# FFN in chunks of 128, 128 and then 256 tokens, w_down loaded in pieces, five weight slabs, and another order of the first loads

## The chip, the cores and the metric

The kernel runs on one core of one Trainium2 chip. The metric is the device time of one execution in microseconds, from the first to the last instruction with what lies around them; a run is one execution, and the time of a kernel is the median of its runs. Profiles come from one further execution.

## The reference

One pre-norm transformer block over 2048 tokens, width 1024, in bf16. Attention has 32 query heads of width 32 that share one key and one value head; the feed-forward part (FFN) has width 3584 and a sigmoid gate.

```python
def _A_ref(x, wq, wk, wv, wo):                 # x: 1 x 2048 x 1024
    q = (x @ wq).reshape(B, S, H, Dh).transpose(0, 2, 1, 3)      # H = 32, Dh = 32
    k = x @ wk
    v = x @ wv
    scores = jnp.einsum("bhqd,bkd->bhqk", q, k) * (Dh ** -0.5)
    p = softmax(scores, axis=-1)
    o = jnp.einsum("bhqk,bkd->bhqd", p, v)
    return o.transpose(0, 2, 1, 3).reshape(B, S, H * Dh) @ wo

def _B_ref(x, w_gate, w_up, w_down):           # F = 3584
    h = sigmoid(x @ w_gate) * (x @ w_up)
    return h @ w_down

h = x + _A_ref(layernorm(x), wq, wk, wv, wo)
out = h + _B_ref(layernorm(h), w_gate, w_up, w_down)
```

## The kernel before

**A planner writes the order.** The kernel doesn't list its instructions by hand. Each operation is an `Op` with an engine, the operations that it depends on, and an assumed cost (`t_act`, `t_dve`, `t_mm`, for DMAs an issue cost `occ` and bytes over a rate). A `Plan` runs a list scheduler over them with those assumed costs, and keeps for each engine one list. When it is done, every engine gets its list as a fixed program, in that order, with semaphore waits where an operation depends on another engine. So the chip follows the planned order whatever the true durations are; an instruction that waits holds up all behind it on its engine. Operations for ACT, DVE, POOL and SP are taken by readiness and then priority. PE's list is made by the loop at line 683, which decides at each moment between a block of scores and other matmuls.

**Tokens** go in 16 tiles of 128. The stages:

- *Head.* x is loaded in 16 tiles into `x_sb` on ACT's DMA queue (line 238), between them wk, wv, the two halves of wq and wo (242 to 260). Per tile (or pair of tiles) DVE takes the statistics (`stats`, line 270), POOL makes the reciprocal deviation with two powers, DVE subtracts the mean (311), and ACT (tiles 1 to 9) or DVE (the others) scales (319, 315). SP then transposes the tile by DMA into `xnT` (322). POOL copies wk four times side by side into `wk4` (266), so that keys come out in four row groups.
- *KV and Q.* `mk_KV` makes keys and values of a pair of tiles, `mk_Q` queries of one group of four heads. The first 512 tokens' queries stay in SBUF (`QTb`), in groups of 256 tokens; the others are made in groups of 512 tokens, copied to `qst` (which lies in `hact`), stored to a DRAM scratch (397) and loaded again per chunk of 256 tokens (416).
- *Attention.* 512 *visits*: for tile and head group (`G` = tile x 8 + group) and a quarter of the keys, `emit_S` issues 16 score matmuls, four at a time in four row groups, and ACT takes two exponentials of 128 x 1024 (line 478). Four visits make one group's probabilities; then `mk_PV` multiplies them by the values (64 matmuls of 33 columns, the last column giving the sum), and DVE divides (511, 513). A tile's eight groups are transposed by DMA into `OT` (519), and `mk_OP` multiplies by wo, adds x, takes the second layer norm's statistics and writes `hn` (302). Visits 0 to 31 belong to tile 0, 32 to 63 to tile 1, and so on, the first two groups interleaved.
- *FFN.* `hn` is transposed by DMA into `hnT` (579), which holds one chunk. For each chunk of 256 tokens (`c`, 8 of them) and each of 28 tiles of F, `mk_GU` does 8 gate and 8 up matmuls of 256 columns into one PSUM bank; ACT takes tanh (620; sigmoid is written with it), DVE multiplies into `hactT` (627). The weights come in *slabs* of 256 columns of F, gate and up, 512 KB each, into a ring of four (`wgu`, `load_slab`, line 588), which all chunks load anew; a slab is loaded when the last matmul on its space is done. `mk_D` then does the down projection, four groups of 28 matmuls of 512 columns, adds h (659) and stores (662).

**Space that is shared.** `wd_sb` (w_down, 7 MB) lies over `zone`, where `xnT`, wq, wk and wv are: it is loaded in four pieces when the last query group is done (line 400). `x_sb` lies over the slab ring: slab s waits until the transposes of tiles 4s to 4s+3 have landed (line 672).

**What may run when.** Two PSUM banks (`F_ps`) serve all groups but the scores. PE takes the first class in `PRIO` whose queue has a group that is ready: KV, Q0, PV, OP, D, GU, Q. A score block goes first if ACT has under 750 ns of work waiting. A chunk's GU groups need all queries done (chunk 0) or the chunk before wholly through D (`gr.gate`, 642); their transposes need both tiles' `hn` and the last GU matmul of the chunk before (`flush_hT`, 576). So chunk c needs tiles 2c and 2c+1 through attention.

The numbers of visits that the prediction uses come from the order of PE's instructions in the built programs. Before: OP of tile 1 ends at visit 72, GU of chunk 0 runs in visits 77 to 120 and its D in 120 to 144, OP of tile 3 ends at 140, chunk 1 starts at 146, chunk 6 at 486. After the last score block stand, in this order: 34 GU matmuls, 64 of PV, 64 GU, 16 OP, 96 GU, 112 D, 448 GU, 112 D.

The softmax here doesn't subtract the row's maximum and nothing guards it: scores larger than these inputs give would overflow.

## Time and profile before

| | us |
|---|---|
| runs | 1210.52, 1211.20, 1210.39 |
| median | 1210.52 |
| the profiled execution's own time | 1211.99 |
| its span, first to last instruction | 1210.2 |
| PE busy | 1148.6 (95%) |
| ACT busy | 1037.1 (86%) |
| DVE busy | 287.8 (24%) |
| ACT: 1024 exponentials, busy | 974.7, 1037 ns each |
| PE: 3584 GU matmuls, busy | 440.8 |
| DMA | 163.56 MB, 135 GB/s over the span |
| DMA queue of ACT (loads of the head) | 8.52 MB |
| slab loads | 224 of 512 KB, all on SP |

Busy time is the time in which an engine has at least one instruction under way; consecutive instructions overlap in their pipelines, so 1037 ns is the length of one exponential, while the spacing of consecutive ones is less. PE's share of 95% says that it almost always has something under way, not that it runs at its peak. The chain of waits follows the work that ended last back from the end, and is the view that says which engine's speed set the end in each stage.

### The profile page before, as it was taken

To read this page: it belongs to the slowest core of one execution; us is meant where nothing else is said; L and a number is where in the kernel's file an instruction comes from. 1 tells how busy PE (TensorE), PEld (TensorE's weight loads), DVE (VectorE), ACT (ScalarE), POOL (GpSimd) and SP (SyncE) were. 2 spreads that over 40 slices of the span, in tenths; PEclk is the share of its full clock that TensorE was granted. 3 is DMA by queue.
4 is the path that set the end of the run, shared out by engine and by line. 5 is a ranking of instruction groups with operands and counts; after the bars stand their busy time and mean duration, and the time that the engine had idled before them with its cause. 6 is when DMAs were issued, how large, how long until landed. Compare 5 with 4: busy or idle time off the path is not lost.

```text
span 1210.2 us, 46354 instructions
## 1 busy us (share of the span) xinstructions
PE 1148.6 (95%) x21632; PEld 812.1 (67%) x21632; DVE 287.8 (24%) x762; ACT 1037.1 (86%) x1281; POOL 39.4 (3%) x86
## 2 busy tenths in 40 slices
PE   0899957999999999999999999999999999999999
PEld 0655545877577866777577866787568865787684
DVE  8222302221122212221212121222122221222121
ACT  1679998999999999999999999999999999991120
POOL 4100000000000000000000000000000000000000
PEclk9999957999999999999999999999999999999999
DMA  9941271666146541657236660576326750569390
GB/s 314 195 97 46 63 263 28 182 159 179 42 117 170 162 129 29 182 152 197 43 83 158 175 154 24 133 195 184 63 63 176 182 141 15 115 177 239 111 251 18
DMA packets 309297, 163.56 MB, mean 135 GB/s; under 512 B 57968, under 2 KB 299632, under 8 KB 309104
## 3 DMA queue, kind: packets, MB, share of 16 engines
q1 hardware_dynamic: 301600, 152.07, 48.8%
q10 hardware_dynamic: 7504, 8.52, 2.1%
q8 instruction: 170, 2.79, 1.0%
q14 instruction: 23, 0.19, 0.1%
HBM read 140.64 MB, written 7.34 MB: 122 GB/s over the span
## 4 chain that ended last, share of the span: by engine, by line
PE 86%; ACT 10%; DMA 2%; ACTq 1%; issue 0%; DVE 0%
PE F_ps L335 73%; PE S_ps L335 13%; ACT Pr L478 9%; DMA zone<-ring 2%; ACTq L238 1%; ACT ring L319 1%; ACTq L249 0%; ACT QTb L228 0%; ACTq L244 0%; DVE h_sb L659 0%; ACT kT L228 0%; ACTq L260 0%; ACTq L242 0%; ACT Vaug L228 0%; ACT L319 0%
## 5 line engine op out<-in xcount | busy, mean ns | idle before, releaser
L478 ACT ACTIVATE Pr<-S_ps 128x1024 bf16<-128x1024 f32 x1024 | 974.7, 1037 | 25.8 <-PE S_ps L335 24.5
L335 PE MATMUL F_ps<-hnT,ring 128*128 128x256 bf16 x3584 | 440.8, 274 | 0.3 <-issue 0.2
L335 PEld LDWEIGHTS F_ps<-hnT,ring 128*128 128x128 bf16 x3584 | 330.3, 98 | 58.8 <-issue 1.0
L335 PEld LDWEIGHTS F_ps<-Vaug,Pr 128*128 128x128 bf16 x8192 | 230.5, 96 | 28.2 <-issue 4.1
L335 PE MATMUL F_ps<-Vaug,Pr 128*128 128x33 bf16 x8192 | 245.0, 178 | 2.5 <-ACT Pr L478 2.4
L335 PE MATMUL S_ps<-QTb,kT 32*128 32x128 bf16 x8192 | 210.4, 220 | 18.7 <-ACT Pr L478 17.5
L335 PE MATMUL F_ps<-zone,hact 128*128 128x512 bf16 x896 | 213.7, 380 | 0.0
L335 PEld LDWEIGHTS S_ps<-QTb,kT 32*128 32x128 bf16 x8192 | 120.6, 94 | 136.7 <-ACT Pr L478 83.5
L627 DVE SCALAR_TENSOR_TENSOR hact<-tnh,F_ps 128x256 bf16<-128x256 f32 x224 | 94.4, 421 | 425.6 <-ACT tnh L620 425.5
L620 ACT ACTIVATE tnh<-F_ps 128x256 f32<-128x256 f32 x224 | 88.1, 393 | 82.3 <-PE F_ps L335 82.3
L335 PEld LDWEIGHTS F_ps<-zone,hact 128*128 128x128 bf16 x896 | 78.9, 98 | 88.3
L335 PE MATMUL F_ps<-zone 128*128 128x512 bf16 (+2 forms) x512 | 76.7, 297 | 36.7 <-DMA zone<-ring 34.7
L335 PEld LDWEIGHTS F_ps<-zone 128*128 128x128 bf16 x512 | 38.5, 100 | 59.2 <-issue 35.3
L659 DVE SCALAR_TENSOR_TENSOR h_sb<-F_ps,h_sb 128x512 bf16<-128x512 f32 x32 | 22.1, 692 | 200.0 <-PE F_ps L335 200.0
L335 PE MATMUL F_ps<-wo_sb,OT 128*128 128x512 bf16 x256 | 65.8, 387 | 0.4 <-issue 0.4
L511 DVE RECIPROCAL rL<-F_ps 128x4 f32<-128x4 f32 x128 | 23.4, 183 | 153.5 <-PE F_ps L335 153.5
L288 POOL TENSOR_SCALAR zb<-mvb 128x1 bf16<-128x1 bf16 (+1 forms) x25 | 5.6, 223 | 1060.1 <-DVE mvb L284 1059.9
L513 DVE TENSOR_TENSOR Osb<-F_ps,rL 128x128 bf16<-128x128 f32 x128 | 37.3, 291 | 4.6 <-DVE rL L511 0.2
L335 PEld LDWEIGHTS F_ps<-wo_sb,OT 128*128 128x128 bf16 x256 | 21.8, 98 | 23.5 <-issue 2.4
L555 DVE TENSOR_TENSOR h_sb<-F_ps,xres 128x512 bf16<-128x512 f32 x32 | 22.1, 692 | 55.2 <-PE F_ps L335 55.2
L229 DVE CAST hact<-F_ps 128x512 bf16<-128x512 f32 x24 | 16.6, 692 | 37.6 <-PE F_ps L335 37.4
L228 ACT ACTIVATE kT<-F_ps 128x256 bf16<-128x256 f32 x7 | 2.8, 393 | 18.1 <-PE F_ps L335 18.1
(27 smaller groups left out, 131.5 us busy)
## 6 DMA issues: line engine op xcount, KB each, us to landing
ring<-in_B_w_gate_dram SPq DMA_DIRECT2D x112, 512.0 KB, 4.2
ring<-in_B_w_up_dram SPq DMA_DIRECT2D x112, 512.0 KB, 5.9
zone<-in_B_w_down_dram SPq DMA_DIRECT2D x4, 1792.0 KB, 15.2
ring<-in_A_x_dram ACTq DMA_DIRECT2D x16, 256.0 KB, 7.6
xres<-in_A_x_dram SPq DMA_DIRECT2D x16, 256.0 KB, 2.6
out_dram<-h_sb SPq DMA_DIRECT2D x32, 128.0 KB, 1.7
q_scratch<-hact SPq DMA_DIRECT2D x24, 128.0 KB, 1.8
QTb<-q_scratch SPq DMA_DIRECT2D x6, 512.0 KB, 3.7
```

Source lines behind the costliest of these rows:

```text
L229: lambda: DVE.tensor_copy(out=out_ap, in_=in_ap))
L238: x_ld[t] = dma(lambda: ACT.dma_start(x_sb[:, t, :], xf[t * P:(t + 1) * P, :]), f"x{t}", P * D * 2, prio=0, ring="act")
L288: f = pl.op("pool", lambda: POOL.tensor_scalar(out=zb[:, ph, sl].unsqueeze(2), in0=mvb[:, ph, sl, 1:2], scalar1=LN_EPS_BF16, scalar2=None, ...
L319: xnorm[t] = pl.op("act", lambda t=t: ACT.activation(out=x_sb[:, t, :], in_=x_sb[:, t, :], func=ACTF.Copy, scale=rstd[:, 0, t:t + 1]), [ce ...
L335: return lambda: PE.matmul(o, lhsT=l, rhs=r, start=start, stop=stop, **kw)
L478: exps[u] = pl.op("act", lambda slot=slot, pb=pb: ACT.activation(out=Pr[:, slot, :].rearrange("p (a b) -> p a b", a=2), in_=S_ps[:, pb:pb ...
L511: a = pl.op("dve", lambda: DVE.reciprocal(rL[:, k, :].unsqueeze(2), ov[:, :, DH:DH + 1]), [last], prio=0, occ=70, lat=280)
L513: e = pl.op("dve", lambda: DVE.tensor_tensor(out=Osb[:, qb % 2, g * P:(g + 1) * P].rearrange("p (a b) -> p a b", a=4), in0=ov[:, :, 0:DH], ...
L555: h_ev[(t, dc)] = pl.op("dve", lambda: DVE.tensor_tensor(out=h_sb[:, t % 4, sl], in0=F_ps[:, b, :], in1=xres[:, t % 2, sl], op=ALU.add), [ ...
L620: a = pl.op("act", lambda: ACT.activation(out=tnh[:, k, :], in_=F_ps[:, b, 0:256], func=ACTF.Tanh, scale=0.5), [last, tn_user.get(k)], pri ...
L627: e = pl.op("dve", lambda: DVE.scalar_tensor_tensor(out=hactT[:, ft, :], in0=tnh[:, k, :], scalar=1.0, in1=F_ps[:, b, 256:512], op0=ALU.ad ...
L659: e = pl.op("dve", lambda: DVE.scalar_tensor_tensor(out=h_sb[:, t % 4, sl], in0=F_ps[:, b, :], scalar=0.5, in1=h_sb[:, t % 4, sl], op0=ALU ...
```

## The change

It does five things.

1. FFN chunks: `CH` is [0], [1], [2, 3], [4, 5], ... [14, 15]: nine chunks instead of eight, the first two of 128 tokens. Their gate and up matmuls have 128 columns, their tanh and product too; each chunk still loads all 14 slab pairs. The gates of GU and of the `hnT` transposes follow the chunk table.
2. w_down comes in seven pieces of 1 MB, each when the part of `zone` under it is free. For that `xnT` is laid out as four blocks of 512 tokens, one behind another; piece i < 4 needs the queries and keys of its 512 tokens, pieces 4 to 6 all queries and keys.
3. Five slabs in the ring instead of four (the fifth first loaded after the last x tile's transpose); `OT` has two buffers instead of four.
4. Loads of the head: x0, x1 and x2 with x3 on SP, the other x tiles in three loads of four tiles on ACT's queue, behind wk and wv; wo moves from ACT's to SP's queue and waits for the load of x12 to x15. A small exponential on ACT takes the table load ahead of the first scaling. The four copies of wk move from POOL to ACT.
5. The planner assumes 520 ns instead of 70 for the issue of a DMA, which reorders the queues.

The order of PE's instructions in the built program after the change: OP of tile 0 ends at visit 40, GU of chunk 0 runs in visits 46 to 79 and its D in 79 to 88; chunk 1: GU 90 to 116, D 117 to 126; OP of tile 3 ends at visit 136, chunk 2 starts at 140, chunk 7 at 482. After the last score block: 37 GU matmuls, 64 of PV, 48 GU, 16 OP, 64 GU, 112 D, 448 GU, 112 D. Ahead of the ninth score block stand all KV groups, all 16 query groups of 256 tokens and four of 512 (before: two). On DVE all statistics of x stand ahead of the first copy out of PSUM. On SP: six transposes of x, the first slab pair, wo, four transposes, four more, half a slab pair, the last two.

```diff
+    CH = [[0], [1]] + [[t, t + 1] for t in range(2, NT, 2)]
+    CHUNK_OF = {t: c for c, ts in enumerate(CH) for t in ts}
+    POS = {t: i for ts in CH for i, t in enumerate(ts)}
-    NSLAB = 4
+    NSLAB = 5
-        OT = SB("OT", [4, NG, P])
+        OT = SB("OT", [2, NG, P])
-        xnT = zview(0, DT, S)
+        xnT4 = [zview(c * DT * 512, DT, 512) for c in range(4)]
+
+        def xnT(dt, a, n):
+            return xnT4[a // 512][:, dt, a % 512:a % 512 + n]
...
-            return pl.op(ring, fn, deps, occ=70.0, key=key, nbytes=nbytes, prio=prio)
+            return pl.op(ring, fn, deps, occ=520.0, key=key, nbytes=nbytes, prio=prio)
...
+        load_x([0], SP, "sp")
+        load_x([1], SP, "sp")
+        load_x([2, 3], SP, "sp")
+        wk_ld = dma(lambda: ACT.dma_start(wk_sb, A_wk.rearrange("(a p) j -> p a j", p=P)), "wk", P * DT * DH * 6, prio=0,
+                    ring="act")
+        wv_ld = dma(lambda: ACT.dma_start(wv_sb, A_wv.rearrange("(a p) j -> p a j", p=P)), "wv", P * DT * DH * 6, prio=0,
+                    ring="act")
+        load_x([4, 5, 6, 7], ACT, "act")
         load_wq(0)
-        for t in range(4, 8):
-            load_x(t)
+        load_x([8, 9, 10, 11], ACT, "act")
+        load_x([12, 13, 14, 15], ACT, "act")
         load_wq(1)
-        for t in range(8, NT):
-            load_x(t)
-        wo_ld = dma(lambda: ACT.dma_start(wo_sb[:, :, :], A_wo.rearrange("(g p) n -> p g n", p=P)), "wo", D * D * 2, prio=1,
-                    ring="act")
+        warm = pl.op("act", lambda: ACT.activation(out=tnh[:, 0, 0:1], in_=half, func=ACTF.Exp), [c0], prio=1, occ=1400)
+        wo_ld = dma(lambda: SP.dma_start(wo_sb[:, :, :], A_wo.rearrange("(g p) n -> p g n", p=P)), "wo", D * D * 2,
+                    [x_ld[12]], prio=4)
...
-            rep = pl.op("pool", lambda r=r: POOL.tensor_copy(out=wk4[:, :, DH * r:DH * (r + 1)], in_=wk_sb),
-                        [wk_ld], occ=400, prio=3)
+            rep = pl.op("act", lambda r=r: ACT.activation(out=wk4[:, :, DH * r:DH * (r + 1)], in_=wk_sb, func=ACTF.Copy),
+                        [wk_ld], prio=1, **t_act(256))
...
-                    for i in range(4):
-                        a, b2 = i * 7, i * 7 + 7
-                        wd_ld.append(dma(lambda a=a, b2=b2: SP.dma_start(
-                            wd_sb[:, a:b2, :], B_w_down[a * P:b2 * P, :].rearrange("(a p) n -> p a n", p=P)),
-                            f"wd{i}", 7 * P * D * 2, [last], prio=4))
...
+        def free_wd(last):
+            for i in list(wd_left):
+                if (i < 4 and q_left4[i] == 0 and 2 * i in k_ev and 2 * i + 1 in k_ev) or \
+                        (i >= 4 and q_left[0] == 0 and len(k_ev) == NT // 2):
+                    wd_left.remove(i)
+                    load_wd(4 * i, 4, [last])
...
-                return all(p in v_ev for p in range(NT // 2)) and (qb < 4 or (qb - 4) in op_last)
+                return all(p in v_ev for p in range(NT // 2)) and (qb < 2 or (qb - 2) in op_last)
...
-            while late_hT and (late_hT[0] < 2 or (late_hT[0] // 2 - 1) in gu_last):
+            while late_hT and (CHUNK_OF[late_hT[0]] == 0 or (CHUNK_OF[late_hT[0]] - 1) in gu_last):
...
-                        r.append((mm(F_ps[:, b, w * 256:(w + 1) * 256], wgu[:, sl, w, dt, fo:fo + P], hnT[:, dt, :],
-                                     dt == 0, dt == DT - 1), 256, [slab_ld[s][w]] if dt == 0 else []))
+                        r.append((mm(F_ps[:, b, w * 256:w * 256 + n], wgu[:, sl, w, dt, fo:fo + P], hnT[:, dt, 0:n],
+                                     dt == 0, dt == DT - 1), n, [slab_ld[s][w]] if dt == 0 else []))
...
-            gr.gate = lambda: s in slab_ld and (q_left[0] == 0 if c == 0 else d_done[c - 1] == 4)
+            gr.gate = lambda: s in slab_ld and (q_left[0] == 0 if c == 0 else d_done[c - 1] == 2 * len(CH[c - 1]))
...
-            load_slab(s, [xT_ev[k] for k in range(4 * s, 4 * s + 4)])
+            load_slab(s, [xT_ev[k] for k in range(4 * s, 4 * s + 4)] if s < 4 else [xT_ev[NT - 1]])
```

## The prediction

> **What bounds the kernel now.** I read four views in this order: the slices of the page (where is an engine not full), a table of windows cut at the places that the slices point to, the chain of work that ended last, and the timeline of ACT and SP in the places that the chain goes through. First the table of windows, whose columns after the window are its length, then busy time and instruction count of PE, PEld, DVE, ACT and POOL, the granted clock, the DMA share and GB/s:

> ```profile
> 0.00:30.50 30.50, 0.00 (x0) 0.01 (x1) 25.43 (x70) 4.51 (x4) 14.28 (x32) 1.00 0.97 315
> 30.50:74.30 43.80, 37.02 (x548) 27.79 (x549) 11.37 (x33) 28.18 (x45) 3.71 (x6) 1.00 0.93 186
> 74.30:151.90 77.60, 77.12 (x1555) 44.31 (x1554) 24.12 (x53) 77.42 (x84) 1.36 (x3) 1.00 0.20 51
> 151.90:202.90 51.00, 31.54 (x832) 21.35 (x832) 6.67 (x21) 48.96 (x54) 1.34 (x3) 0.64 0.51 171
> 346.00:483.00 137.00, 137.00 (x2770) 97.84 (x2768) 29.94 (x82) 134.16 (x165) 2.69 (x6) 1.00 0.49 129
> 1086.00:1210.00 124.00, 121.27 (x926) 85.64 (x924) 26.44 (x58) 15.20 (x40) 1.34 (x3) 1.00 0.64 159
> ```

> So there are four regimes: a head in which PE does nothing for 30.5 us and then starves on and off until 74 us; a stretch to 203 us with ACT full, whose last 51 us leave 19.5 us of PE empty at a clock of 0.64; a long middle with both engines full; and 124 us after attention in which PE alone works. The chain tells what ends each (start, length, who):

> ```profile
> 4.07 3.07 ACTq L249
> 18.41 11.87 DMA zone<-ring
> 30.52 5.72 PE F_ps L335 x40
> 49.48 5.11 DMA zone<-ring
> 61.42 5.00 DMA zone<-ring
> 109.86 14.89 ACT Pr L478 x16
> 245.68 1.85 PE F_ps L335 x16
> 253.95 1.76 PE F_ps L335 x43
> 1083.68 123.61 PE F_ps L335 x946
> ```

> The head hangs on DMA transposes (zone<-ring), which hang on ACT's queue. In the third regime the chain is one exponential after another: 14.89 us for 16, so 0.931 us each, and 1.862 us for a visit (one block of scores, two exponentials). In the middle the chain is PE: four visits take from 245.68 to 253.95, 8.27 us or 2.07 a visit, as long as gate and up matmuls run beside them; during the down projection the exponentials set 1.864 again. One 256-token chunk takes 68 visits and 137.2 us (the same D-to-attention pattern of the chain starts at 300.02, 437.08 and 574.44). The end is PE from 1083.68 to the last output.

> Three groups and one timeline give the prices:

> ```profile
> L335 PE MATMUL F_ps<-Vaug,Pr 128*128 128x33 bf16 x8192 | 245.0, 178 | 2.5 <-ACT Pr L478 2.4
> L620 ACT ACTIVATE tnh<-F_ps 128x256 f32<-128x256 f32 x224 | 88.1, 393 | 82.3 <-PE F_ps L335 82.3
> L335 PEld LDWEIGHTS F_ps<-hnT,ring 128*128 128x128 bf16 x3584 | 330.3, 98 | 58.8 <-issue 1.0
> 1134.03 49.07 PE L335 MATMUL F_ps<-hnT,ring 128*128 128x256 bf16 x448
> ```

> **Head: fewer loads, wo later.** ACT's first computation is at 15.95 us, because it issues 19 DMAs before (most take 0.46 us of its sequencer, one 3.07). Afterwards it issues seven, with 3 MB of x and the same two wq loads. At the same excess (0.92 for wv, 3.07 behind it) that is about 8 us; then the table load (1.28) and four copies of wk, which move from POOL (1.6 us in all there) to ACT, at most 4 x 0.39. So ACT is ready near 11.5 us instead of 17.24, and the three scalings of tiles 1 to 3 end at about 17.5 instead of 20.5, held by DVE's statistics, which are full from 4.5 us on and stay.

> The larger part is the bandwidth. ACT's queue moved 8.5 MB, until 30.3 us, at 327 to 381 GB/s in stretches of 5 us; tiles 1 to 3 were issued for transposing from 18.41 on and landed as it ended (18.41 + 11.87 = 30.28). wo is 2 MB of it and now waits for the last x and behind six transposes on SP; taking it out ends the loads 2.1 MB / 0.36 = 5.8 us earlier. I put PE's start at 30.5 - 5.8 = 24.7 us; bounds: 22 (if the scalings alone held it) and 30.5 (if transposes still drain last).

> From there to the ninth visit PE has, by the built order, 8 key/value groups (8 x 1.3), 16 query groups of 256 (16 x 0.87), 4 of 512 (8 x 0.214 each), 9 score blocks (0.4 each) and one value product (1.7): 36 us. Two more groups than before stand ahead of it (2 x 1.7). Before, it took 74.3 - 30.5 = 43.8 us for 33 us of work. Now there is one wait to pay that I can see: SP issues one slab pair and wo (3 MB) ahead of transposes 6 to 9, on the same ring, so these go about 9 us later than they could, near 41 us; PE has eleven query groups (9.6 us) in front of the first that needs them, so most is covered, and 3 us of waiting for transposes 4 and 5 remain. DVE no longer stops: before, its last statistics stood behind a copy that waits for PE (idle 15.4 us before the copy at 50.77); now all its statistics come first. Ninth visit: 24.7 + 36 + 3 = 64 us against 74.3: **-10.3** (bounds -16 and 0).

> **Stretch to visit 140.** Both orders reach the fourth output projection there; before, by counting the exponentials in the timeline, visit 8 is at 74.3 and visit 140 at 333.45, 259.1 us. Of this 132 x 1.862 = 245.8 are exponentials, 28 tanh at 0.27 us (from 1059.76 to the exponential at 1060.03) are 7.6, and 5.7 are lost in transitions and in the slow clock. After, chunk 0 runs in visits 46 to 79 and chunk 1 in 90 to 116, where PE had been empty; ACT pays 56 tanh of 128 columns. No row shows that shape; the 64-column copy takes 250 ns and the 256-column one 393, so an occupancy of 0.11 to 0.27, and by the slope of these rows 0.16: 9.0 us, +1.4 (bounds -1.4, +7.5). A chunk in the middle loses 137.2 - 68 x 1.862 - 7.6 = 3.0 us in its transitions; two chunks 6, the gap that is left in visits 126 to 136 about 1.3: 7.3 against 5.7. Sum **+3** (bounds -2 and +10).

> What PE pays there: 896 matmuls of 128 columns instead of 448 of 256. The trace has none over full rows; 33 columns cost 245.0 / 8192 = 30 ns with their weight load and 256 columns 49.07 / 448 = 109, so between; nearest by streaming is half of the second, 54 ns: the same PE time. In a visit of chunk 0 that is 13.6 x 0.054 + 0.97 for scores and values = 1.7 us, of chunk 1 17.2 x 0.054 + 0.97 = 1.9, both under ACT's 2.0. [...]

> The gap in visits 126 to 136 matters for the clock:

> ```profile
> 150.00:160.00 10.00, 5.84 (x200) 4.54 (x196) 1.05 (x5) 9.91 (x12) 0.00 (x0) 0.80 0.95 329
> 160.00:170.00 10.00, 5.12 (x148) 3.71 (x144) 0.47 (x2) 9.91 (x12) 0.00 (x0) 0.50 1.05 389
> 190.00:200.00 10.00, 7.51 (x217) 5.17 (x215) 4.71 (x12) 9.93 (x11) 1.34 (x3) 1.00 0.12 30
> ```

> Some 6 us after PE falls to half load the grant goes to 0.50, although no pause there is over 1.6 us. I expect the same in the new gap, 19 us long: the output projection's 16 matmuls take 0.43 instead of 0.21 us, 3.4 us, of which the two slow places of before (2.3 us a visit around visit 68, 2.5 around 76) cost as much. [...]

> The further 28 slab loads (14.7 MB) need 14 x 1.05 MB in visits 46 to 90 (some 88 us): 167 GB/s; the last chunk of before drew 286 GB/s with PE at 30.00 of 30 us. Five slabs instead of four cost nothing but space. w_down, 7 MB, comes in seven pieces instead of four; four of them still go at the end of the queries, 24 us before the first slab that could be late behind them. OT with two buffers waits for an output projection that lies 30 visits back.

> **From visit 140 on.** Both have 372 visits and seven 256-token chunks left. Before, chunk 1 starts at visit 146, now its like at 140; so at the last score block 149 gate and up matmuls of the next-to-last chunk remain instead of 194. The 45 come out of the tail, 45 x 0.109 = **-4.9 us**, and stand under attention at 2.07 instead of 1.864 us in six more visits: **+1.2**. Here PE's empty 19.5 us go: not into the end, since chunk 2 can't start before the fourth tile's attention, which ACT sets.

> **Sum.** -10.3 + 3 + 1.2 - 4.9 = -11.0 us. The profiled execution took 1211.99 us (span 1210.2 and 1.8 around it), so 1201.0; the median of the three runs is 1.5 under the profiled one: **1199.5 us**.

> **Rivals.**
> - *The head stays.* The transposes 6 to 15 wait so long behind slab and wo that visit 9 is at 74 again. For it: three of the chain's pieces there are transposes. Against: 3 MB are 9 us, with 9.6 us of queries in front. Time 1199.5 + 10.3 = 1210. Chance 0.13.
> - *The empty PE time is recovered.* If the middle were PE's alone and chunks could slide forward, the 19.5 us would come off the middle as well: 1199.5 - 14 = 1185.5 (some is used by then). For it: the chain is PE in the middle. Against: the order still puts chunk 2 at 140. Chance 0.15.
> - *Slower: 128-column matmuls are held by their weight load.* For it: the PEld row, 98 ns a load. Against: value products at 30 ns with the same 128x128 load. At 98 ns a visit of chunk 0 takes 2.3 and of chunk 1 2.66 us of PE: 33 x 0.3 + 26 x 0.6 = 26 us, 1226. It outweighs the gain from about 80 ns on. Chance 0.10, with slabs that come too late counted in, which would show in the same visits.
> - That the main case holds: 0.62, 1192 to 1208.

> **Range.** 1188 to 1209: from the head at its best (-16) and the stretch without loss to a head that gains little. About 0.2% (2.4 us) is what a measurement here can tell. Faster than 1208.1: the main case, the recovery and a little of the first rival, 0.79; within: 0.10; slower: 0.11.

> **What would show it.** Right: first matmul near 25 us, ninth visit near 64, the exponentials in visits 46 to 116 at 2.0 us a visit, no PE wait for slabs in chunks 0 and 1, some 118 us from the last score block to the end. Wrong: a DMA wait of over 5 us before PE between 35 and 60 us; visits of chunk 1 over 2.2 us; a middle chunk that is not 137 us.

## The result, and the profile after

The changed kernel is slower: 1220.43 us (median of 4 runs, 1219.12 to 1224.75) against 1210.66 us for the kernel before on the same chip (4 runs), a ratio of 1.0086 with a 95% interval of 1.0061 to 1.0112. The forecast was 1199.5 us, and its range ended at 1209. The profiled execution took 1220.96 us, its span 1219.1 against 1210.2 before.

The table puts the loss in its place. It gives the start of the first exponential of some visits, read from the records of ACT, and so the length of each stretch.

| stretch, us | before | after | difference | forecast |
|---|---|---|---|---|
| first matmul at | 30.5 | 25.0 | -5.5 | -5.8 |
| start to visit 8 | 74.3 | 69.3 | -5.0 | -10.3 |
| visits 8 to 12 | 7.5 | 12.9 | +5.4 | in the next row |
| visits 12 to 140 | 251.6 | 264.2 | +12.6 | +3 |
| visits 140 to 511 | 750.3 | 751.1 | +0.8 | +1.2 |
| from there to the end | 126.5 | 121.6 | -4.9 | -4.9 |
| span | 1210.2 | 1219.1 | +8.9 | -11 |

So three rows went wrong, all ahead of visit 140, by 5.3, 5.4 and 9.6 us. The windows of the changed kernel, in the columns explained above, cut at these visits:

```profile
0.00:25.00 25.00, 0.03 (x1) 0.06 (x2) 20.90 (x59) 5.83 (x9) 11.20 (x25) 1.00 1.04 311
25.00:69.30 44.30, 38.58 (x562) 28.75 (x566) 15.87 (x44) 29.25 (x48) 5.65 (x9) 1.00 0.96 223
69.30:82.20 12.90, 9.69 (x146) 4.98 (x147) 2.01 (x5) 7.60 (x8) 0.00 (x0) 0.74 0.80 206
152.00:214.80 62.80, 53.60 (x1293) 43.72 (x1295) 11.37 (x42) 54.23 (x80) 0.00 (x0) 0.90 1.03 265
358.00:495.00 137.00, 135.82 (x2750) 97.65 (x2757) 30.07 (x82) 134.20 (x165) 2.68 (x6) 1.00 0.48 128
```

A middle chunk (fifth row) is what it was. In the stretch of chunk 0 (fourth row) PE is no longer half empty: it has 53.60 us of work. But 9 us of PE are still empty, ACT is not full either (54.23 of 62.80), and the DMA share is at 1.03. Neither engine is the bound there, so something else stops both. The chain of waits of the first 330 us names it:

```profile
1.84 9.02 DMA ring<-in_A_x_dram
14.72 10.01 DMA zone<-ring
46.59 4.23 DMA zone<-ring
56.44 4.97 DMA zone<-ring
70.36 2.73 issue
145.02 8.69 DMA q_scratch<-hact
160.29 1.28 issue
204.56 2.75 issue
251.81 2.40 issue
285.72 1.64 issue
```

(These are its pieces that matter here, not all.) "Issue" is time in which an engine waited for nothing that the profile shows. Such pieces of over a microsecond are new: the chain of before has none of this length from its first matmul on. PE's timeline shows where the longest one falls (start, length, what, and in brackets the idle time ahead with its cause):

```profile
203.62 0.94 PE L346 MATMUL F_ps<-Vaug,Pr 128*128 128x33 bf16 x31
207.31 0.27 PE L346 MATMUL F_ps<-Vaug,Pr 128*128 128x33 bf16 x4 [2.75 <-issue]
```

PE stops in the middle of one group of 64 value products, between the 60th and the 64th, all of whose inputs were there when the group began. PE's waits from 150 to 310 us sum it up (us in total, times, longest), first of the changed kernel:

```profile
PE F_ps L346 <- issue: 6.1, 7, 2.7
PE S_ps L346 <- issue: 4.8, 4, 2.4
PE S_ps L346 <- ACT Pr L503: 3.6, 6, 1.6
PE F_ps L346 <- DVE hact L654: 2.4, 4, 1.1
```

and of the kernel before:

```profile
PE S_ps L335 <- ACT Pr L478: 17.5, 19, 1.4
PE F_ps L335 <- ACT Pr L478: 2.4, 5, 0.6
```

Before, PE only ever waits for ACT there, which costs nothing while ACT is full (48.96 of the 51.00 us from 151.9 to 202.9). After, 10.9 us are "issue", and no wait is for a slab: the weights were not late.

The traces say more than these four stops do. Some matmul records are missing (92 of 22,080 here), so a place in the program is better counted by weight loads, each with its matmul, and semaphore instructions. By that count the twelve traces of this case have 47 "issue" stops of over 0.5 us inside a group of matmuls, and every one stands 194 or 195 past a multiple of 256 (so do two more, at the first matmul of a group). The changed program has 173 such places, and 173 of these packets ran; the program before has 170, and 170 ran. So one packet belongs to each place. From PE's passing a place to the start of its packet it takes 0.4 us (median of 61 in the changed kernel) where the DMA share in the 3 us around it is under 0.3, and 2.7 us (24) where it is over 1.1. Ahead of these 49 stops it took 2.0 to 4.8 us, and PE went on 2.2 to 3.1 us after the packet's start: by theory A it stops where the two together are longer than its work on a block.

Why the forecast passed over the stops is seen in two windows with the DMA engines equally full, the first from the tail of the kernel before, the second from chunk 0 after:

```profile
1150.00:1160.00 10.00, 10.00 (x94) 8.96 (x92) 2.53 (x6) 2.25 (x6) 0.00 (x0) 1.00 1.17 290
170.00:180.00 10.00, 8.87 (x229) 7.70 (x224) 2.20 (x9) 9.10 (x15) 0.00 (x0) 1.00 1.13 289
```

At 1150 PE gets through 186 instructions in 10 us, a block in 13.8 us, and never stops. At 170 it is 453, a block in 5.7 us, and it does. Between the two lies the kernel before from 700 to 710 us: 348 instructions, a share of 1.11, and no stop. The forecast read from the first kind of row that such traffic is free.

### The profile page after: what moved, and what is told of

Read it like the earlier page. It is cut to its first block, busy times and chain, and to the rows that moved or that the text cites. A ratio compares the mean times of both kernels' runs of the same rounds, so it can differ in the third digit from the quotient of the medians.

```text
span 1219.1 us, 47282 instructions
## 1 busy us (share of the span) xinstructions
PE 1143.3 (94%) x21988; PEld 820.6 (67%) x22080; DVE 289.2 (24%) x788; ACT 1041.3 (85%) x1316; POOL 38.4 (3%) x82
## 4 chain that ended last, share of the span: by engine, by line
PE 85%; ACT 7%; issue 3%; DMA 3%; DVE 1%; ACTq 0%; DVEq 0%
PE F_ps L346 72%; PE S_ps L346 13%; ACT Pr L503 6%; DMA zone<-ring 2%; DMA ring<-in_A_x_dram 1%; DMA q_scratch<-hact 1%; ACT tnh L647 1%; ACT ring L330 1%; DVE hact L654 0%; DMA hnT<-hn 0%; DVE st L285 0%; DVE st L287 0%; DVE h_sb L580 0%; ACT QTb L235 0%; DVE mv L289 0%
## 5 line engine op out<-in xcount | busy, mean ns | idle before, releaser
L346 PE MATMUL F_ps<-hnT,ring 128*128 128x256 bf16 (+1 forms) x4032 | 445.9, 262 | 4.7 <-issue 1.6
L346 PEld LDWEIGHTS F_ps<-hnT,ring 128*128 128x128 bf16 x4032 | 340.6, 98 | 61.3 <-issue 5.9
L346 PE MATMUL S_ps<-QTb,kT 32*128 32x128 bf16 x8192 | 208.8, 218 | 18.5 <-ACT Pr L503 10.9
L346 PE MATMUL F_ps<-zone,hact 128*128 128x512 bf16 x843 | 203.2, 380 | 3.8 <-issue 1.8
L654 DVE SCALAR_TENSOR_TENSOR hact<-tnh,F_ps 128x256 bf16<-128x256 f32 (+1 forms) x252 | 97.7, 391 | 445.0 <-ACT tnh L647 436.6
L647 ACT ACTIVATE tnh<-F_ps 128x256 f32<-128x256 f32 (+1 forms) x252 | 94.5, 380 | 81.3 <-PE F_ps L346 81.3
L346 PE MATMUL F_ps<-zone 128*128 128x256 bf16 (+2 forms) x497 | 73.2, 294 | 31.9 <-DMA zone<-ring 26.6
L346 PE MATMUL F_ps<-wo_sb,OT 128*128 128x512 bf16 x232 | 60.7, 390 | 4.1 <-issue 2.1
L306 POOL TENSOR_TENSOR rstd<-dsb,cst 128x1 f32<-128x1 bf16 (+1 forms) x25 | 16.7, 667 | 1.9
## 6 DMA issues: line engine op xcount, KB each, us to landing
ring<-in_A_x_dram ACTq DMA_DIRECT2D x3, 1024.0 KB, 12.6
```

The costliest lines, as they stand in the source:

```text
L306: h = pl.op("pool", lambda: POOL.tensor_tensor(out=rstd[:, ph, sl], in0=dsb[:, ph, sl], in1=nb, op=ALU.pow), [g, c1], prio=prio - 1, occ=5 ...
L346: return lambda: PE.matmul(o, lhsT=l, rhs=r, start=start, stop=stop, **kw)
L647: a = pl.op("act", lambda: ACT.activation(out=tnh[:, k, 0:n], in_=F_ps[:, b, 0:n], func=ACTF.Tanh, scale=0.5), [last, tn_user.get(k)], pri ...
L654: e = pl.op("dve", lambda: DVE.scalar_tensor_tensor(out=hactT[:, ft, 0:n], in0=tnh[:, k, 0:n], scalar=1.0, in1=F_ps[:, b, 256:256 + n], op ...
```

## The experiments

Times are medians, ratios are to the kernel before on the same chip with their 95% intervals; visit times come from one profiled execution each.

**1. Without slab loads 5 to 27.** The 46 loads of these 23 slab pairs and the waits on them are left out; the order of everything else is unchanged.

```diff
+            if 5 <= s < 28:
+                for o in ops:
+                    o.ghost = True
...
             for o in lists[e]:
+                if o.ghost:
+                    continue
...
-                    if d.eng == e and e == "pe":
+                    if (d.eng == e and e == "pe") or d.ghost:
                         continue
```

> The changed kernel with the slab loads 5 to 27 left out (chunk 0 from its sixth slab on and the whole of chunk 1 multiply by whatever the ring holds); every engine's order is otherwise the same. Theory A (the weight traffic of the two half chunks fills the DMA engines, and TensorE's own instruction blocks arrive late behind it): the stops of TensorE in the middle of matmul groups between 155 and 300 us go, visits 56 to 140 take 171 to 173 us instead of 178.8, time 1211 to 1213 us. Theory B (the slabs themselves arrive late): the same. Theory C (the half chunks cost this by themselves: twice the tanh, the order, the slow clock): visits 56 to 140 stay at 177 or more, time 1218 to 1222.

1211.56 us, ratio 1.0003 (0.9992 to 1.0013). PE's waits from 150 to 310 us:

```profile
PE S_ps L347 <- ACT Pr L504: 6.8, 15, 1.6
PE F_ps L347 <- DVE hact L658: 1.0, 2, 0.7
```

Every "issue" stop in this stretch is gone, and visits 12 to 140 take 254.4 us, +2.8 on before, where the forecast said +3. So the forecast's price of the half chunks was right in its sum, and 264.2 - 254.4 = 9.8 us belong to the slab loads. Theory C falls; between A and B the run can't decide. The stop near 73 us, ahead of these loads, stays (2.37 us).

**2. The same traffic, which nobody reads.** The same 46 loads as copies from the weights to a scratch area in device memory, with no wait on them.

```diff
+            if 5 <= s < 28:
+                for w, o in enumerate(ops):
+                    o.ghost = True
+                    o.fn = (lambda w=w, W=W: SP.dma_start(
+                        junk[s - 5, w].rearrange("(a p) f -> p a f", p=P),
+                        W[:, pi * SW:(pi + 1) * SW].rearrange("(a p) f -> p a f", p=P)))
...
```

> As the kernel without those slab loads, but in place of each a copy of the same bytes from the weights to a DRAM scratch, issued at the same place on SP and waited for by nobody. Theory A: the stops come back, in the middle of groups and a multiple of 256 TensorE instructions apart, some 2.6 us after a 16 KB instruction packet starts; visits 56 to 140 take 175 us or more, time 1215 to 1221. Theory B: nobody waits for these bytes, so visits 56 to 140 stay at 171 to 173 and the time at 1211 to 1213.

1218.9 us, ratio 1.0064 (1.0046 to 1.0082). Visits 12 to 140 take 262.6 us, 8.2 of the 9.8 back, without one wait on a slab (on the medians, against run 1 on the same chip, 7.3 us). Stops stand at the numbers 5057, 6337 and 6593, 5 and 1 times 256 apart. Late slabs are out as the cause; it is the traffic itself.

**3. Chunks of 256 only.** All of the change but its half chunks.

```diff
-    CH = [[0], [1]] + [[t, t + 1] for t in range(2, NT, 2)]
+    CH = [[t, t + 1] for t in range(0, NT, 2)]
```

> The changed kernel with eight chunks of 256 tokens again; head, w_down pieces, five slabs and planner stay changed. Theory A: the stop in visits 8 to 12 stays (it stands behind the slab and w_down loads of the head), visit 12 at 82 us; visits 12 to 140 take 251 to 253 us as in the kernel before, the tail is as long as before; time 1209 to 1212. Rival (the loss of visits 48 to 140 comes from the loads' order and the planner, not from the half chunks): time 1216 or more.

1212.57 us, ratio 1.0018 (1.0007 to 1.003), 0.6 us over theory A's range and far under the rival's. From visit 12 on it is the kernel before (visit 140 at 333.9 us against 333.4, tail 126.5 in both). Its one stop inside a group, 2.0 us, ends at 73.7; visit 8 is at 70.7, visit 12 at 81.7 (81.9 before). So the whole gain of the head is given back within four visits, half chunks or not.

**4. Half chunks alone,** put into the kernel before (w_down in four pieces, four slabs, the old head).

```diff
-    NC = NT // 2
+    CH = [[0], [1]] + [[t, t + 1] for t in range(2, NT, 2)]
...
-            gr.gate = lambda: s in slab_ld and (q_left[0] == 0 if c == 0 else d_done[c - 1] == 4)
+            gr.gate = lambda: s in slab_ld and (q_left[0] == 0 if c == 0 else d_done[c - 1] == 2 * len(CH[c - 1]))
```

> The kernel before with the chunks of 128, 128 and then 256 tokens alone. Theory A: visit 12 at 82 us as before; the last query store stands behind all 7 MB of w_down, and the first product of chunk 0 waits for it, so visits 48 to 60 lose 5 to 10 us; then the same stops as in the changed kernel; tail 5 us shorter; time 1219 to 1228. Rival (half chunks are harmless, the other parts cost the time): 1203 to 1208.

1228.94 us, ratio 1.0144 (1.0114 to 1.0175). Visits 48 to 56 alone take 26.3 us (14.8 before). The time is 0.9 us over theory A's range. The chain names a second thing, which the expectation has and the prediction had not seen:

```profile
151.31 7.25 SPq L406
158.61 13.88 DMA q_scratch<-hact
```

SP first issues w_down, 7 MB, and then the last query store, which lands 13.88 us after it was issued. DVE's first product of chunk 0 overwrites the space that this store reads (`q_store` among its dependences), so it waits. In the changed kernel the same wait stands at 145.02 (8.69 us): the smaller pieces of w_down shorten it but don't remove it.

**5. All query stores ahead of the last four pieces of w_down,** in the changed kernel, by moving entries of SP's list.

```diff
+        late = [o for o in sp if o.key in ("wd12", "wd16", "wd20", "wd24")]
+        sp[:] = [o for o in sp if o not in late]
+        at = max(i for i, o in enumerate(sp) if o.key is not None and o.key.startswith("qs")) + 1
+        sp[at:at] = late
```

> The changed kernel with SP's list alone reordered: the last four w_down pieces stand behind the last query store instead of two before and two around it. If the first product of chunk 0 is held by a store that waits behind w_down on the ring, DVE's wait for the store (8.3 us) falls under 2 us and visits 48 to 56 take 15 to 16 us instead of 18.2; time 2 to 3 us less, 1216 to 1219. If something else holds it, 18 us stay.

1218.46 us, ratio 1.0058 (1.0038 to 1.0078). The wait for the store is gone, but visits 48 to 56 go only from 18.2 to 17.6 us: a stop of 1.10 us that ends at 161.59 is still there. The store was mostly hidden behind other delays; in this kernel it is worth about half a microsecond. That part of the theory failed, although the time lies in its range.

**6. Slabs 3 and 4 and the first piece of w_down spread** between the query stores, in the changed kernel.

```diff
+        late = [[o for o in sp if o.key in ks][:len(ks)] for ks in (("sl30", "sl31"), ("sl40", "sl41"), ("wd0",))]
...
+        for g, n in reversed(list(zip(late, (3, 7, 11)))):
+            sp[qs[n] + 1:qs[n] + 1] = g
```

> The changed kernel with SP's list alone reordered: slabs 3 and 4 and the first w_down piece, which stood in one burst with slabs 1 and 2 before 75 us, go one by one behind later query stores. Theory A (TensorE's instruction block is late behind the burst): the stop of 2.9 us near 73 us goes, and with it the slow clock behind it; visits 8 to 12 take 7.5 to 9 us instead of 12.9; time 1213 to 1216. Rival (the stop comes from something in TensorE's own work): 12.9 us stay and the time is 1218 to 1222.

1213.94 us, ratio 1.0031 (1.002 to 1.0043). No stop near 73 us; visits 8 to 12 take 7.6 us as before (12.9 after), visit 12 is at 77.8 us. So the second wrong row of the table is the stop and the slow clock behind it, and the loads that crowd there (a DMA share of 1.17 and 1.19 in the 5 us before and after 70 us in the changed kernel) cause it. The profile (span 1208.4) is of the fastest of its seven executions, 3.8 us under their median, and so flatters it.

**7 and 8. All 16 transposes ahead of wo and slabs,** with chunks of 256 (7) and with the change's chunks (8); both with the stores of run 5.

```diff
+        plan = [(1, ("wo",)), (3, ("sl00", "sl01")), (5, ("sl10", "sl11")), (8, ("sl20", "sl21")), (10, ("sl30", "sl31")),
+                (13, ("sl40", "sl41")), (17, ("wd0",))]
...
+        for n, g in reversed(late):
+            sp[qs[n] + 1:qs[n] + 1] = g
```

> Eight chunks of 256 tokens with the changed head; SP's list reordered: all sixteen transposes of x before wo and all slabs, these spread behind the query stores, the last w_down pieces behind the last store. If wo and the slabs on the ring ahead of the transposes took the head's gain: visit 8 at 61 to 65 us, visit 12 at 69 to 73 (before 81.9), then as before; time 1198 to 1203. If the scalings and statistics hold the transposes instead: visit 12 at 76 or later, time 1204 to 1210.

> The changed kernel, chunks of 128, 128 and then 256 tokens, with the same reordering of SP's list. The head and the wait for the store gain as in the run with pairs; the stops of chunks 0 and 1 stay, about 8 us, against a tail that is 5 us shorter: time 2 to 6 us over the run with pairs, 1201 to 1207.

Run 7: 1210.94 us, ratio 1.0005 (0.9997 to 1.0014). Run 8: 1216.77 us, ratio 1.0049 (1.0035 to 1.0062). Both miss their expectations: run 7 lies over both of its ranges, and run 8 some 10 us over its own, though 5.8 us over run 7 is inside the 2 to 6 that it named. Visit 8 comes at 67.9 and 68.1 us; the six traces with the order of the change there (the changed kernel, runs 1, 2, 3, 5 and 6) have 69.3 to 71.7. So transposes that wait behind slab and wo were worth 1 to 4 us, not 5 or more. PE is then nearly always at work from 42 us on (25.72 of the 25.90 us to visit 8 in run 7), so what remains is its own work. In run 7 a stop still falls at 70.28, just after wo and slab 0:

```profile
65.00:70.00 5.00, 4.00 (x126) 3.31 (x125) 1.16 (x3) 3.57 (x4) 0.00 (x0) 1.00 1.04 370
70.00:75.00 5.00, 4.38 (x62) 2.22 (x63) 0.47 (x2) 2.24 (x3) 0.00 (x0) 0.66 0.77 223
```

The stop costs twice: PE stands still for 1.3 us, and then the granted clock is at 0.66. (Both profiles are of the fastest execution, 1.8 and 4.7 us under the median.) Run 8 against run 7 is the price of the half chunks with all else equal: 5.8 us on the medians, although the tail is 4.9 us shorter.

**9 and 10. Bursts in another place.** All runs so far use one stretch of one schedule. To try theory A where nothing of the change is, four bursts of copies were put into down projections of the kernel before, on GpSimd's queue (run 10). In it and in its base (run 9) plain copies stand in place of the 48 DMA transposes, so that its matmuls work on tiles that are not transposed.

```diff
-                xT_ev[t] = dma(lambda t=t: SP.dma_start_transpose(
-                    out=xnT[:, :, t * P:(t + 1) * P], in_=x_sb[:, t, :]), f"xT{t}", P * D * 2, [xnorm[t]], prio=0)
+                xT_ev[t] = dma(lambda t=t: SP.dma_start(
+                    xnT[:, :, t * P:(t + 1) * P], x_sb[:, t, :].rearrange("p (a b) -> p a b", a=DT)), f"xT{t}", P * D * 2, [xnorm[t]], prio=0)
...
+        for c in (2, 3, 4, 5):
+            for j in range(6):
+                o = Op("pool", lambda c=c, j=j: POOL.dma_start(
+                    junk[c, j].rearrange("(a p) f -> p a f", p=P),
+                    B_w_up[:, j * SW:(j + 1) * SW].rearrange("(a p) f -> p a f", p=P)), [gu_last[c]], [], 0, 0, 0, 0, "junk", 1)
...
```

> The kernel before, in which the 48 DMA transposes (of x, of the attention output and of the second norm's output) are plain copies of the same tiles from SBUF to SBUF, so that the matmuls get tiles that are not transposed; number, shape and order of all other instructions stay. It is the base for the run with bursts. Every theory: no stop of TensorE inside groups of matmuls after 310 us, as in the kernel before; a middle chunk takes 137 us as there, since transposes lie off the path in the middle; the head may be some us longer or shorter, by how long a copy takes instead of a transpose.

> The run with copies for transposes, to which four bursts are added: when the gate and up matmuls of chunks 2, 3, 4 and 5 have ended, GpSimd's queue issues six copies of 0.5 MB each from the up weights to a scratch area in device memory (12 MB in all). Nobody waits for them, they write nothing that is read, and SyncE's queue and every wait stay as they were. The places are down projections, in which TensorE was at 10.00 of 10 us in the kernel before, with a DMA share under 0.4. Theory A (transfers that fill the 16 DMA engines make TensorE's own 16 KB instruction packets arrive late): TensorE stops inside groups of matmuls, where it waits for no semaphore, at positions that lie a multiple of 256 instructions apart, one to three stops of 0.6 to 3 us in each burst, and the span is 4 to 20 us longer than in the run without bursts. Rival B (the stops of the changed kernel came from its half chunks, its order or its slabs): no stop, spans within 2 us of each other. Rival C (the copies hold up slab loads on the other queue): TensorE waits for a slab's semaphore at the start of a group, after the burst, and not inside groups.

The base: 1211.65 us, ratio 1.0001 (0.9992 to 1.0011). With bursts: 1218.2 us, ratio 1.0057 (1.004 to 1.0074); the spans are 1210.8 and 1216.6. The same window, in the base and with the second burst, and PE's timeline in the latter:

```profile
710.00:720.00 10.00, 9.88 (x221) 6.43 (x217) 1.73 (x6) 8.39 (x10) 0.00 (x0) 1.00 0.36 100
```

```profile
710.00:720.00 10.00, 7.27 (x187) 5.14 (x187) 1.17 (x3) 7.46 (x8) 1.55 (x2) 1.00 1.03 355
```

```profile
706.25 5.31 POOL L740 DMA_DIRECT2D junk<-in_B_w_up_dram  x6 [52.89 <-PE F_ps L336]
716.88 0.44 PE L336 MATMUL F_ps<-Vaug,Pr 128*128 128x33 bf16 x11
720.02 0.20 PE L336 MATMUL F_ps<-Vaug,Pr 128*128 128x33 bf16 x2 [2.69 <-issue]
```

Eleven microseconds after the first copy is issued PE stops for 2.69 us, again within a group of value products. Three of the four bursts bring a stop that the base has not: they end at 578.76, 720.02 and 869.60, 2.4 to 2.5 us after an instruction packet starts (576.33, 717.56, 867.13). Counted by weight loads as above, their places are 21187, 26819 and 32707, which lie exactly 22 and 23 times 256 apart and again 195 past a multiple of it. The fourth burst brought none. The base has one stop of its own after 310 us, against the expectation: 0.98 us, ended at 831.88, at such a place too (31426), with a DMA share of 0.90 in the 5 us ahead; the run with bursts has it as well (0.99). The stretch of chunk 3's burst (visits 276 to 344) grew by 4.6 us for its one stop: the granted clock, 1.00 in the base from 720 to 730, is 0.83 there, and ACT is busy for 6.62 us instead of 9.98. No half chunk, no fifth slab and no order of the change is in this run; rival B falls. Rival C falls too: no wait for a slab shows.

## Why the prediction was wrong, and where it was right

**Right: PE's start, the end, and the half chunks' own price.** First matmul 25.0 us (24.7 forecast; which of the changes to the loads brought it was not separated, and the prediction's 19 DMAs of ACT ahead of its first computation are 21 in the timeline, which changes nothing). Visits 140 to 511 +0.8 us (+1.2), tail -4.9 (-4.9); so PE's empty time was not recovered, and that rival is out. In the new gap (visits 126 to 136) the grant went to 0.50, as forecast, for 6.8 us (321.5 to 324.9 and 328.3 to 331.7). In visits 46 to 116, forecast at 2.0 us each, run 1 has 2.01 and the changed kernel 2.19. That run 1's +2.8 meets the forecast's +3 is in part luck: 2.3 of it stand in visits 48 to 56, with the wait for the store and a clock of 0.50, which the forecast had not there, and 0.3 in visits 56 to 140. Two groups by shape give the price of chunk 0 and 1:

```profile
L346 PE MATMUL F_ps<-hnT,ring 128*128 128x128 bf16 x896 | 60.6, 221 | 2.5 <-issue 1.0 <-DVE hact L654 0.8
L647 ACT ACTIVATE tnh<-F_ps 128x128 f32<-128x128 f32 x56 | 17.3, 332 | 2.4 <-PE F_ps L346 2.4
```

The 221 and 332 ns are the lengths of single instructions, which overlap, and steps are shorter. From start to start the matmuls are 55.9 ns apart in a full stretch (30 of them from 163.15 us on, the first step of 66 ns left out; 54 forecast), and the next exponential starts 0.157 us after a half tanh where ACT is full (0.16 forecast). So the rival of matmuls held by their weight load, at 98 ns, did not happen. That its 1226 us lie nearer to the measured time than the forecast is luck: its other condition, late slabs, did not happen either. None of the prediction's signs of being wrong came (chunk 1 took 2.16 us a visit, a middle chunk 137 us, and no DMA wait of 5 us stood before PE from 35 to 60 us): they looked for what the prediction knew of.

**Wrong: the further 28 slab loads were put at nothing.** The prediction compared a mean demand of 167 GB/s with the 286 GB/s that the last chunk had drawn beside a full PE. Two things were passed over. The loads don't come at their mean: while they run, the DMA share is 1.04 to 1.20 in five of the six windows of 10 us from 150 to 210 us. And the last chunk's row shows PE with 186 instructions in 10 us; at the 453 of the half chunks, the same traffic stops PE. Priced at 0, it measured 9.8 us (run 1), 8.2 of which came back with traffic that nobody waits for (run 2).

**Wrong: the head's -10.3.** This is as large: visit 12, forecast 10.3 us earlier, is where it was, so either step alone would have brought the time to the end of the range or over it (1209.3 with the slab loads, 1210.2 with the head). Two terms. The work ahead of the ninth visit was sized at 36 us with 3 us of waiting, 39; the window from 25.00 to 69.30 has 38.58 us of busy PE and 5.7 empty, 44.3. The prediction's own first table gave a hint: it has PE busy for 37.02 us where the sum counts 33 us of work. Even with the transposes ahead of all (run 7) it was 67.9 - 25.05 = 42.9. And the gain was thought of as kept once PE has it: between visits 8 and 12 a stop of 2.73 us with the slow clock behind it (0.74 on the mean) took 5.4 us back (3.5 to 4.0 in the traces of runs 1, 2, 3 and 5). Run 6 has neither. So these stops, with the slow clock behind some of them, took 12 to 15 of the 21 us between forecast and result. The rival "the head stays" came near in its result, since visit 12 is where it was, though not the ninth visit; it was wrong in its way: transposes behind slab and wo were worth 1 to 4 us.

**Too small to decide: w_down "24 us before the first slab that could be late".** The step looked at slabs and not at the query store that stands behind w_down on the same queue, and at the product that waits for it: 8.3 us of DVE's time in the changed kernel, worth half a microsecond of the whole (run 5); in run 4, with w_down in larger pieces, it is the longest part of the 26.3 us.

**Open.** That a packet holds the next block, and that PE asks for it on passing a place, is inferred from the equal numbers of places and packets, from the times between them and from the four runs with traffic taken away or added; the request itself is in no record. Why the packets start later beside full engines (2.7 us after the place instead of 0.4), while they take little longer (1.15 to 1.75 us ahead of the four stops, against a median of 1.15), was not shown. Visits 48 to 56 keep 1.1 us over the forecast's 16 even without slabs (17.1 in run 1), with the clock at 0.50 beside them; its cause was not separated. A version with chunks of 256 in which no weight is loaded before visit 12 was not tried; no version that ran is faster than the kernel before.

## What to carry to other kernels

Where a profile says "issue" in the middle of a group of matmuls, look at the DMA share there and count instructions. In the twelve traces here, PE stopped only at the end of blocks of 256 that take it under 6 us without the stop (over some 43 instructions in a microsecond): of 225 such blocks whose first 3 us had a DMA share of 0.9 or more 45 ended in a stop of over 0.5 us, of 306 slower ones none, and of the 1095 with a share under 0.6 none. So price added traffic by the share that it reaches while it runs and by how fast the engine beside it uses up instructions, not by its mean rate or by a row with larger matmuls. And when work is cut into smaller pieces that load the same weights again, the extra loads and the denser instructions fall into the same stretch (here a DMA share of 1.13 and 453 instructions from 170 to 180 us).

## What the hardware showed that was not expected

- TensorE stops of 0.5 to 2.75 us at places a multiple of 256 instructions apart, each ending 2.2 to 3.1 us after a 16,384-byte instruction packet starts; for 45 of 49 the DMA share was 0.9 or more in the 3 us after PE passed the place before, for the other four 0.6 to 0.9. The packet itself starts 0.4 us after PE passes a place where the share is under 0.3, and 2.7 us after it where the share is over 1.1 (medians of the changed kernel).
- Some stops were followed by a slow clock, others not. After those of 2.73 and 2.75 us in the changed kernel the grant was 0.50 for 6.8 us (72.3 to 79.1 and 205.4 to 212.2 us), and after 1.28 us in run 7 it was 0.66 over 5 us; after 2.40 us, ended at 254.21, it stayed at 1.00.
- In run 4 a store of 128 KB that stood behind 7 MB of loads on its queue landed 13.88 us after its issue.
- Some kernels with such stops spread more from one execution to the next: 8.5 us over nine executions (run 8) and 7.2 over five (run 5), against 4.3 over 24 of the kernel before; the run with bursts spreads by 1.5 over four. Whether the stops' number differs between executions was not shown.
